# The last group's output stage: adds from bank C moved behind the fifth product, and two stores cut by column halves

## The chip, the cores and the metric

The kernel runs on one core of a Trainium2 chip. The metric is the device time of one execution in microseconds (us). The median of three runs before the change is 302.48 us (302.23 to 303.44).

## What is computed

Sliding-window causal attention over 8 batches, 8 heads, 576 positions and 64 values per head, followed by a feed-forward block on the joined heads:

```python
scores = scale * np.matmul(q, k.transpose(0, 1, 3, 2))      # window of 64, causal
attn   = softmax(masked scores)
x      = heads of attn @ v, side by side                    # [8, 576, 512]
xn     = (x - mu) / np.sqrt(var + 1e-06) * g_ln
ch     = np.maximum(xn @ w_ch1, 0.0) @ w_ch2                # 512 -> 2048 -> 512
out    = x + ch                                             # float32
```

## The kernel before, in words

The 8 x 576 rows are worked off in nine groups of 512 rows. Groups 0 to 7 hold the first 512 rows of one batch each. The ninth group, `g == NGRP - 1`, holds the last 64 rows of all eight batches: its block `kb` (128 rows, one row per SBUF partition) has the last 64 rows of batch `2*kb` in partitions 0 to 63 and those of batch `2*kb + 1` in partitions 64 to 127. The attention result of a block lies in `x_norm[(g, kb // 2)]`, a float32 tile of 128 partitions, 2 blocks and 512 columns; the feed-forward result is added into it in place, and it is stored from there.

The order on each engine is the order in which the program is written (the schedule is manual); nothing is reordered by a planner. Each engine works its own list from top to bottom and waits where an instruction needs another engine's result. Transfers are issued from SyncE's queue (SP) and from ScalarE's (ACT).

For the second matrix product of the block, groups from 2 on use a scheme of seven half-size products in the place of eight. The 512 rows are split in two halves of rows (blocks 0 and 1; blocks 2 and 3) and the 512 output columns in two halves of 256. Sums of the left factor's quarters, `S1` to `S4`, are made by VectorE (`s_sums`, L530); sums of the weights lie ready in `wT`. A product runs in two parts `p`, one per block, of 8 matmuls each, and goes to one of three sums in PSUM:

- bank A takes products 1, then 6, then 7 on top of one another
- bank B takes product 2, later product 4 anew
- bank C takes product 5, then product 3 on top. In the last group it is two separate banks of 256 columns, one per `p`

For the last group the plan runs the products in the order 1, 2, 6, 5, 7, 4, 3. As soon as a bank's sum is right for some part of the output, VectorE adds it into `x_norm` (`post`, L569, takes two blocks at 256 columns; `post_c`, L573, takes one block at 256 columns). A and C for the upper columns, A and B for the lower: blocks 2 and 3 get their upper 256 columns from product 7's A and product 5's C, and their lower 256 columns from product 7's A and product 4's B. Blocks 0 and 1 get their upper columns from product 6's A and product 3's C, which is the last sum of all. `stage(n, p)` runs one part of product `n` and then, after the second part, the adds and stores that it allows; `store_rest` (L511) issues two transfers, one from SP for partitions 0 to 63 and one from ACT for partitions 64 to 127 (or both from one given engine), for the two blocks and the given columns.

Between the parts of the products the plan writes the sums:

```python
stage(5, 0)
s_sums(0, 4, 4)
stage(5, 1)
s_sums(4, 8, 4)
for n in (7, 4, 3):
    for p in range(2):
        stage(n, p)
```

`S4`, of which the two calls here make the two halves, is the left factor of product 3.

Of the kernel before, what the change touches and what calls it, by code (L numbers as in the profile page):

```python
# [18 lines left out]
def kernel(  # L19
# [12 lines left out]
    DM = H * D  # L32
# [437 lines left out]
    def mlp_units(g, split=0, three=False, seven=True):  # L470
# [37 lines left out]
        def store_rest(k0, cols, eng):  # L508
            xv = x_norm[(g, k0 // 2)]
            for r in range(2):  # L510
                (eng or (nc.sync, nc.scalar)[r]).dma_start(  # L511
                    out=out[2 * k0 + r:2 * k0 + r + 3:2, SM:S, cols].rearrange("k s d -> s k d"),
                    in_=xv[64 * r:64 * r + 64, :, cols],
                )

        def store(kb):
            nc.sync.dma_start(out=out[g, 128 * kb:128 * kb + 128, :], in_=x_norm[(g, kb // 2)][:, kb % 2, :])
# [16 lines left out]
        def product(n, p):  # L534
            which, a, wv = {
                1: ("A", hv[:, :, 0, 0:256], w2v[:, :, 0, 0, :]),
                2: ("B", hv[:, :, 1, 0:256], w2v[:, :, 1, 0, :]),
                6: ("A", sS[2], wT[2]),
                5: ("C", sS[1], w2v[:, :, 0, 1, :]),
                7: ("A", sS[3], wT[3]),  # L540
                4: ("B", hv[:, :, 1, 256:512], wT[4]),
                3: ("C", sS[4], w2v[:, :, 1, 1, :]),
            }[n]
            first = n in (1, 2, 5, 4)
            if p == 0 and n in (1, 2 if last else 4, 5):
                if which == "C" and last:
                    for r in range(2):
                        bank[("C", r)] = ps_t.tile([128, 256], FP32, tag=f"t{r}", name=f"pC{r}_{g}")
                elif which == "C":
                    bank[which] = ps_t.tile([128, 2, 256], FP32, tag="t1", name=f"p{which}_{g}")  # L550
                else:
                    bank[which] = ps_mm.tile([128, 2, 256], FP32, tag="mm", name=f"p{which}_{g}")
            split_c = last and which == "C"
            o = bank[(which, p)][:, :] if split_c else bank[which][:, p, :]
            for c in range(NHC // 2):
                nc.tensor.matmul(  # L556
                    out=o, lhsT=a[:, c, 128 * p:128 * p + 128], rhs=wv[:, c, :],
                    start=(first and (p == 0 or split_c) and c == 0), stop=(c == NHC // 2 - 1), skip_group_check=True,
                )

        def post_both(which, kb0):
            xv = x_norm[(g, kb0 // 2)][:, :, :].rearrange("p k (f d) -> p k f d", f=2)
            a = bank[which][:, :, :]
            twice = bass.AP(tensor=a.tensor, offset=a.offset, ap=[a.ap[0], a.ap[1], [0, 2], a.ap[2]])
            nc.vector.tensor_tensor(out=xv, in0=twice, in1=xv, op=ALU.add)

        def post(which, kb0, f):
            xv = x_norm[(g, kb0 // 2)][:, :, 256 * f:256 * f + 256]
            nc.vector.tensor_tensor(out=xv, in0=bank[which], in1=xv, op=ALU.add)  # L569

        def post_c(kb0, r):
            xv = x_norm[(g, kb0 // 2)][:, r, 256:512]
            nc.vector.tensor_tensor(out=xv, in0=bank[("C", r)], in1=xv, op=ALU.add)  # L573

        last = g == NGRP - 1

        def stage(n, p):
            product(n, p)
            if last and n == 3:
                post_c(0, p)  # L580
                if p:
                    store_rest(0, slice(256, DM), None)
                return
            if p == 0:
                return
            if n == 1:
                post("A", 0, 0)
            elif n == 2:
                post("B", 0, 0)
                if last:  # L590
                    store_rest(0, slice(0, 256), nc.sync)
            elif n == 6:
                post("A", 0, 1)
            elif n == 5 and not last:
                post("C", 2, 1)
            elif n == 7 and last:
                post("A", 2, 1)
                post_c(2, 0)
                post_c(2, 1)
                post("A", 2, 0)  # L600
            elif n == 7:
                post_both("A", 2)
                store(2)
                store(3)
            elif n == 4:
                post("B", 2, 0)
                if last:
                    store_rest(2, slice(0, DM), None)
            elif n == 3:
                post("C", 0, 1)  # L610
                tbank["shared"] = False
                tbank["n"] = 0
                store(0)
                store(1)
# [109 lines left out]
        if last:  # L724
            def plan():
# [3 lines left out]
                for d in range(1, 4):  # L729
# [4 lines left out]
                    if d == 2:  # L734
                        s_sums(0, 4, 1)
                stage(1, 0)
                s_sums(0, 4, 2)
                l1_c(3)
                s_sums(4, 8, 1)
                stage(1, 1)  # L740
                l1_e(3)
                s_sums(4, 8, 2)
                stage(2, 0)
                stage(2, 1)
                stage(6, 0)
# [188 lines left out]
    for g in range(NGRP):  # L934
# [171 lines left out]
        n = g + 2  # L1106
# [75 lines left out]
```

## Time and profile before

| what | value |
|---|---|
| median of three runs | 302.48 us (302.23 to 303.44) |
| the profiled execution, its own time | 302.3 us |
| its span, first to last instruction | 300.3 us |
| TensorE busy | 292.2 us (97% of the span) |
| VectorE busy | 208.4 us (69%) |
| ScalarE busy | 153.9 us (51%) |
| GpSimd busy | 158.4 us (53%) |
| mean granted TensorE clock | 0.995 |
| last group's stores (L511) | 6 transfers: 4 from SP's queue, 2 from ACT's |

The profile is of one execution. Its times are counted from the span's start. PE is TensorE's matmul row, PEld its weight loads, DVE VectorE, ACT ScalarE, POOL GpSimd, SP SyncE; SPq and ACTq are the queues' issues of transfers. In a timeline row the columns are start, length, engine, line and operation, output and inputs, shape, and count; neighbouring instructions of one kind are merged, and what stands in brackets is idle time of the engine just before and what ended it. Ends of matmuls are modelled.

### The profile page before, as it was taken

Reading aid. Unit: us, or ns where it says so; the run is one execution under the profiler, and the core shown is the slowest. Engines: PE = TensorE matmul, PEld = TensorE weight load, DVE = VectorE, ACT = ScalarE, POOL = GpSimd, SP = SyncE. Lnnn points to the kernel's source line nnn. Section 1 sums busy time; section 2 is a strip of 40 time slices with the busy share of each in tenths; the row PEclk is TensorE's granted clock in tenths of the full one; section 3 lists DMA queues with packets and bytes.
Section 4 is the critical chain, followed back from the end, with each engine's and each line's share of the span. In section 5 each row is a group of like instructions: output and inputs, shape, how many; then the busy total and the mean of one; then the engine's idle time right before and its main releaser. Section 6 shows DMA issues by size and latency. Waiting matters only on the chain.

```text
span 300.3 us, 7568 instructions
## 1 busy us (share of the span) xinstructions
PE 292.2 (97%) x3067; PEld 195.6 (65%) x3067; DVE 208.4 (69%) x409; ACT 153.9 (51%) x259; POOL 158.4 (53%) x234
## 2 busy tenths in 40 slices
PE   8989999999999999999999999999999999999992
PEld 3557545887544588557854786469646854788881
DVE  1781338865937985488858865698667775879972
ACT  2666646676458525873276438841674056216400
POOL 4787877634633876278518860797048307115200
PEclk9999999999999999999999999999999999999997
DMA  7999999989979998999289999992639396013014
GB/s 191 260 382 335 384 286 289 269 266 306 134 194 297 206 187 128 290 248 177 53 265 289 195 160 270 297 163 48 212 72 157 70 232 146 10 38 121 0 38 105
DMA packets 114020, 58.34 MB, mean 194 GB/s; under 512 B 83649, under 2 KB 104705, under 8 KB 113986
## 3 DMA queue, kind: packets, MB, share of 16 engines
q1 hardware_dynamic: 113696, 57.47, 80.0%
q8 instruction: 24, 0.39, 0.6%
q10 hardware_dynamic: 290, 0.40, 0.5%
q14 instruction: 10, 0.08, 0.1%
HBM read 38.80 MB, written 9.44 MB: 161 GB/s over the span
## 4 chain that ended last, share of the span: by engine, by line
PE 95%; ACT 1%; DVE 1%; issue 0%
PE hps L479 31%; PE pA L556 12%; PE pB L556 8%; PE pC L556 8%; PE hph L621 7%; PE ch L491 6%; PE xps L387 4%; PE sc L340 4%; PE ch L638 4%; PE tp L267 3%; PE lA L677 2%; PE warm L848 2%; PE lC L677 1%; PE ztp L456 1%; PE lB L677 1%; ACT pt L350 1%
## 5 line engine op out<-in xcount | busy, mean ns | idle before, releaser
L479 PE MATMUL hps<-zT,w1g 128*128 128x512 f16 x416 | 94.7, 379 | 0.0
L483 ACT ACTIVATE hrT<-hps 128x512 f16<-128x512 f32 x104 | 62.3, 599 | 41.2 <-PE hps L479 37.8
L479 PEld LDWEIGHTS <-w1g 128*128 128x128 f16 x416 | 39.2, 98 | 45.5 <-issue 2.2
L350 ACT ACTIVATE pt<-sc 128x512 f16<-128x512 f32 x72 | 39.3, 600 | 21.4 <-PE sc L340 20.7
L556 PEld LDWEIGHTS <-sS 128*128 128x128 f16 x448 | 43.3, 98 | 5.0
L431 POOL TENSOR_SCALAR rsz<-mvg 128x1 f32<-128x1 f32 x28 | 9.7, 347 | 67.7 <-DVE mvg L412 65.7
L360 DVE TENSOR_TENSOR pt<-pt,mask 128x1024 f16<-128x1024 f16 x32 | 24.7, 776 | 22.3 <-ACT pt L350 22.3
L145 POOL CAST qk<-qk 128x1024 f16<-128x1024 f32 x30 | 33.0, 1114 | 10.3 <-PE hph L621 4.5
L556 PEld LDWEIGHTS <-hrT 128*128 128x128 f16 x336 | 32.1, 98 | 6.4 <-ACT hrT L483 1.0
L248 ACT COPY qkT<-tp 128x1024 f16<-128x1024 f16 (+1 forms) x18 | 17.4, 964 | 24.7 <-PE tp L267 22.4
L556 PE MATMUL pC<-w2s,sS 128*128 128x256 f16 x224 | 26.9, 273 | 0.0
L556 PE MATMUL pA<-wT,sS 128*128 128x256 f16 x224 | 26.9, 273 | 0.0
L407 DVE TENSOR_TENSOR xn<-xps,rcp 128x256 f32<-128x256 f32 (+1 forms) x50 | 25.8, 539 | 1.2 <-DMA out_dram<-xn 0.5
L409 DVE BATCH_NORM_STATS2 stats<-xn 128x6 f32<-128x512 f32 x36 | 25.0, 695 | 1.2
L530 DVE TENSOR_TENSOR sS<-hrT 128x512 f16<-128x512 f16 (+1 forms) x40 | 24.1, 604 | 1.9 <-ACT hrT L483 1.8
L621 PE MATMUL hph<-zT,w1g 128*128 128x256 f16 x192 | 23.4, 273 | 0.1
L437 POOL TENSOR_SCALAR z<-xn,rsz 128x512 f16<-128x512 f32 x24 | 20.7, 862 | 2.5
L403 DVE RECIPROCAL rcp<-xps 128x4 f32<-128x4 f32 (+1 forms) x50 | 7.9, 181 | 18.4 <-PE xps L387 18.4
L432 POOL TENSOR_TENSOR rsz<-rsz,mhalf 128x1 f32<-128x1 f32 x28 | 18.7, 670 | 2.3
L621 PEld LDWEIGHTS <-w1g 128*128 128x128 f16 x192 | 18.1, 98 | 2.9 <-issue 0.2
L491 PE MATMUL ch<-w2s,hrT 128*128 128x512 f16 x80 | 18.8, 380 | 0.0
L387 PEld LDWEIGHTS <-pt 128*64 128x64 f16 x576 | 11.6, 110 | 10.3 <-issue 6.0
(119 smaller groups left out, 427.9 us busy)
## 6 DMA issues: line engine op xcount, KB each, us to landing
out_dram<-xn SPq DMA_DIRECT2D x33, 256.0 KB, 3.2
qk<-in_q_dram SPq DMA_DIRECT2D x16, 512.0 KB, 6.2
qk<-in_k_dram SPq DMA_DIRECT2D x16, 512.0 KB, 7.2
v<-in_v_dram SPq DMA_DIRECT2D x28, 256.0 KB, 6.3
w2s<-in_moe_w_ch_dram SPq DMA_DIRECT2D x9, 512.0 KB, 8.6
w1s<-in_moe_w_ch_dram SPq DMA_DIRECT2D x4, 512.0 KB, 7.2
tk<-in_k_dram SPq DMA_DIRECT2D x8, 256.0 KB, 4.4
tv<-in_v_dram SPq DMA_DIRECT2D x8, 256.0 KB, 4.8
```

Source lines behind the costliest of these rows:

```text
L145: nc.gpsimd.tensor_copy(out=dst[:, :].rearrange("p (a j) e d -> p a e j d", j=j), in_=t[:, :].rearrange("p (a e j d) -> p a e j d", e=2, j ...
L350: nc.scalar.activation(out=o, in_=i, func=AF.Exp, bias=0.0, scale=scale)
L360: nc.vector.tensor_tensor(out=ptv, in0=ptv, in1=mb, op=ALU.mult)
L387: nc.tensor.matmul(out=tiles[h // n][64 * r:64 * r + 64, h % n, :D + 1], lhsT=pt[:, par, hp, r, :], rhs=rhs, start=True, stop=True)
L407: nc.vector.tensor_tensor(out=xn[:, n * i:n * i + n], in0=xps[:, :, 0:D], in1=rcp_b, op=ALU.mult)
L409: nc.vector.bn_stats(out=stats, in_=xv)
L479: nc.tensor.matmul(out=hps, lhsT=w1g[:, kc, 128 * hc:128 * (hc + 1)], rhs=zT[g][:, kc, :], start=(kc == 0), stop=(kc == NKC - 1),)
L483: nc.scalar.activation(out=hrT[:, hc, :], in_=hps, func=AF.Relu, bias=0.0, scale=1.0)
L491: nc.tensor.matmul(out=ch[kb], lhsT=hrT[:, hc, 128 * kb:128 * (kb + 1)], rhs=w2s[:, hc, :], start=(hc == 0), stop=(hc == NHC - 1),)
L530: nc.vector.tensor_tensor(out=o, in0=x, in1=y, op=op)
L556: nc.tensor.matmul(out=o, lhsT=a[:, c, 128 * p:128 * p + 128], rhs=wv[:, c, :], start=(first and (p == 0 or split_c) and c == 0), stop=(c ...
L621: nc.tensor.matmul(out=hps[:, e], lhsT=w1g[:, kc, 128 * hc:128 * (hc + 1)], rhs=zT[g][:, kc, 256 * half:256 * half + 256], start=(kc == 0) ...
```

## The change

In the last group, the two adds of C into blocks 2 and 3 are issued after the second part of product 5 and no longer after product 7. The store of these two blocks' 512 columns, which followed product 4's add, becomes two: the upper 256 columns are stored after product 7's first add, the lower 256 after product 4's add. Each is again one transfer from SP and one from ACT. Nothing else differs, in the other groups neither.

```diff
-            elif n == 5 and not last:
+            elif n == 5 and last:
+                post_c(2, 0)
+                post_c(2, 1)
+            elif n == 5:
                 post("C", 2, 1)
             elif n == 7 and last:
                 post("A", 2, 1)
-                post_c(2, 0)
-                post_c(2, 1)
+                store_rest(2, slice(256, DM), None)
                 post("A", 2, 0)
...
             elif n == 4:
                 post("B", 2, 0)
                 if last:
-                    store_rest(2, slice(0, DM), None)
+                    store_rest(2, slice(0, 256), None)
```

## The prediction

> **What bounds the kernel now.** I read the chain that ended last first, then the same chain for the last twelve microseconds, then the timeline there, and then the stores (issues with time to landing, and traffic by stretch). Over the whole span the chain is TensorE:
>
> ```profile
> PE 95%; ACT 1%; DVE 1%; issue 0%
> ```
>
> The change touches only the last group's output stage, so what counts is how that chain ends. From 289 us on it reads (start, length, what):
>
> ```profile
> 289.35 1.75 PE pA L556 x16
> 291.10 1.75 PE pB L556 x16
> 292.85 1.76 PE pC L556 x16
> 294.61 0.02 issue
> 294.63 0.42 DVE xn L573
> ```
>
> Products seven (pA), four (pB) and three (pC) run back to back, 1.75 us each; the last add follows 0.02 us after and ends at 295.05. No compute follows, but the span ends at 300.3: 5.25 us, about 1.7% of it, are stores. The timeline of that stage:
>
> ```profile
> 288.85 1.29 DVE L530 TENSOR_TENSOR sS<-hrT,sS 128x1024 f16<-128x1024 f16 x2
> 291.14 0.69 DVE L569 TENSOR_TENSOR xn<-pA,xn 128x512 f32<-128x512 f32 x1 [1.00 <-PE pA L556]
> 291.86 0.76 DVE L573 TENSOR_TENSOR xn<-pC,xn 128x256 f32<-128x256 f32 x2
> 292.54 0.68 DVE L569 TENSOR_TENSOR xn<-pA,xn 128x512 f32<-128x512 f32 x1
> 293.32 0.69 DVE L569 TENSOR_TENSOR xn<-pB,xn 128x512 f32<-128x512 f32 x1
> 293.93 0.41 DVE L573 TENSOR_TENSOR xn<-pC,xn 128x256 f32<-128x256 f32 x1
> 294.04 1.64 SPq L511 DMA_DIRECT2D out_dram<-xn  x2
> 294.04 1.91 ACTq L511 DMA_DIRECT2D out_dram<-xn  x2
> 294.63 0.42 DVE L573 TENSOR_TENSOR xn<-pC,xn 128x256 f32<-128x256 f32 x1 [0.28 <-PE pC L556]
> ```
>
> VectorE stands idle for 1.00 us before 291.14 and is then full until 294.34; the adds of blocks 2 and 3 from C (the two at 291.86) sit in the full part. Both halves of those rows go out at 294.04 in one pair of transfers (SP and ACT, 256 KB each), and the last pair (128 KB each) follows at 295.08. Of these four, in the order SP, ACT, SP, ACT (bytes each, us from issue to landing):
>
> ```profile
> out_dram<-xn SPq DMA_DIRECT2D x1, 256.0 KB, 3.2
> out_dram<-xn ACTq DMA_DIRECT2D x1, 256.0 KB, 4.5
> out_dram<-xn SPq DMA_DIRECT2D x1, 128.0 KB, 3.9
> out_dram<-xn ACTq DMA_DIRECT2D x1, 128.0 KB, 4.1
> ```
>
> The last lands at 295.08 + 4.1 = 299.2; 1.1 us of program end follow. SyncE's queue waits for exactly that:
>
> ```profile
> SPq L1177 <- DMA out_dram<-xn: 3.5, 1, 3.5
> ```
>
> And the transfers are busy, not merely late. By stretch (last two columns: share of the DMA engines, GB/s):
>
> ```profile
> 290.00:295.20 5.20, 4.59 (x43) 3.87 (x40) 3.63 (x8) 0.00 (x0) 0.00 (x0) 1.00 0.00 0
> 295.20:296.70 1.50, 0.00 (x0) 0.00 (x0) 0.00 (x0) 0.00 (x0) 0.00 (x0) 1.00 0.90 180
> 296.70:298.90 2.20, 0.00 (x0) 0.00 (x0) 0.00 (x0) 0.00 (x0) 0.00 (x0) 0.57 0.79 235
> ```
>
> For 5.2 us nothing moves; then 768 KB go in some 3.6 us, with the last pair queued behind the 512 KB of the pair before it. That queue is what the change can shorten.
>
> **The change, part by part.**
>
> *The two adds of C for blocks 2 and 3.* They move ahead of the second half of the last sum S4, to behind product five. Product five's end is product seven's start in the chain, 289.35. The first half of S4 fills VectorE until 288.85 + 0.64 = 289.5, so neither add waits; they take 0.76 us (their row at 291.86), and the second half of S4 ends at about 289.5 + 0.76 + 0.69 = 290.95 instead of 290.14. Behind it on VectorE is the add from A, due at 291.14, and still in time. The only other one who waits for S4 is product three, at 292.85: 1.9 us of slack, and PE loses nothing. The cover is the idle 1.00 us before 291.14; without it the 0.76 us would delay the A add as now, and reach PE only if more than 1.9 us.
>
> *VectorE behind product seven.* The A add for the upper half runs 291.14 to 291.83, as now. The A add for the lower half follows at once, 291.8 to 292.5. The add from B is then late on PE, not on VectorE: pB ends at 292.85, so it runs about 292.9 to 293.6 instead of 293.32 to 294.01. The first last C add needs half of product three (292.85 + 0.88 = 293.73) and the second needs all of it: 294.63 to 295.05, unchanged. So 0.76 us leave VectorE's full stretch and nothing of this reaches the last add; the worth of it is only the earlier release of stores.
>
> *The stores.* The pair of 256 KB becomes two pairs of 128 KB. The upper halves go at about 291.87, the lower halves at 293.6, the last pair at 295.08 as before. Added: one issue on SP's queue and one on ACT's, by their rows 0.6 us each on SP (two in 1.64 us with a gap) and up to 0.9 on ACT (two in 1.91). ACT's and SP's queues hold nothing else then, and the middle pair's issue ends by 294.5, 0.6 us ahead of the last one. Nobody waits behind them.
>
> *What the last pair finds in front of it.* Now 512 KB, issued 1.0 us earlier. Then 256 KB, issued 1.5 us earlier; the upper halves move in a stretch that shows 0 GB/s today. From issue to first bytes is about 1.2 us (294.04 to the traffic's start at 295.2). Two ways to price it:
> - By the row of a pair that finds nothing in front: its second half, ACT's 256 KB, landed after 4.5 us. A pair of half the size has 256 KB less to move, 1.46 us at 180 GB/s or 1.12 us at 235: landing after 3.0 to 3.4 us. Against 4.1 that is 0.7 to 1.1 us won. A 128 KB store of the same shape, issued alone at 286.61, landed after 3.2 us, which lies inside.
> - What may be taken off: the middle pair lands by the same figure at 293.6 + 3.0 to 3.4 = 296.6 to 297.0, and the last pair's first bytes come at 295.08 + 1.2 = 296.3. Some 0.0 to 0.4 us of queue stay, the landing itself including a receipt of about 0.3 us (traffic ends at 298.9, landing 299.2).
>
> So 0.3 to 1.1 us are won; I take 0.9, the 3.2 us of the nearest row (same shape and size). Sum: span 300.3 - 0.9 = 299.4, the profiled execution 302.3 - 0.9 = 301.4. That execution lies 0.2 us under the median of the runs, 302.48, so the median becomes 301.6.
>
> *Packets of half the length.* A row's run in DRAM falls from 2 KB to 1 KB. The pair at 286.61 has 1 KB runs; the stretch 287.9 to 289.7, which holds all its traffic, shows 146 GB/s at a DMA share of 0.64, against 180 at 0.90 for 2 KB runs. Per busy share that is 228 against 200: no loss shows. Bound: 256 KB at 146 GB/s, 1.8 us, against 1.46 at 180, so 0.3 us later for the last pair if it queues, which stays inside the 0.3 to 1.1.
>
> [...]
>
> **The rivals.**
>
> *The last landing does not move* (chance 0.18). ACT's transfer of a pair landed 1.3 us after SP's though both were issued at 294.04. If that lag belongs to the second queue and not to the bytes, the ACT half lands 4.1 us after 295.08 with whatever in front. For: ACT's lag also shows with an empty queue. Against: the last pair's lag is only 0.2 us. Time: 302.5.
>
> *More than a measurement can tell* (0.14). The lag is all queue, and with little in front the last pair lands as fast as the fastest store in the kernel: 2.0 us (the minimum over all output stores; median 3.3). Then 2.1 us are won: 300.4. Against: no store of the 64-row shape landed under 3.2.
>
> *Slower* (0.06). A transfer costs by its number, not its bytes: the first 256 KB transfer kept the engines from 295.2 to about 296.7, 1.5 us. Six transfers at 1.5 us in series from 293.1 (291.87 + 1.2) end at 302.1 instead of 298.9, 3.2 us later: 305.7. It decides from 0.97 us each (293.1 + 6 x 0.97 = 298.9). Against: the two transfers at 286.61 together fit in 1.8 us.
>
> That the change doesn't do what it says could only be that the early C adds wait for product five; by 289.35 against 289.5 they don't, and the slack of 1.9 us covers it.
>
> **How the numbers follow.** The forecast has 0.62. About 0.5% of the time, 1.5 us, is what a measurement of this kernel can tell from no change; that puts the bounds at 301.0 and 304.0. The forecast (301.4 to 302.2) and the first rival are within; 0.02 of the forecast's 0.62 may fall below 301.0 by scatter, while 0.01 of the rival "more" stays above it: faster 0.15. Slower by over 0.5% comes from the last rival alone, 0.06. Same is 0.79. Range: 300.6 to 302.8 holds the forecast and the first rival with the runs' scatter (302.23 to 303.44 before), and leaves out the two other rivals, 0.2.
>
> **What would show it.** Right: the chain's last C add still at 294.6, PE without a new gap before product three, traffic from about 293.1, a pair issued at 293.6, the last landing after 3.0 to 3.4 us. Wrong: PE waiting for S4, the first A add behind 291.2, the last issue later than 295.1, or a last landing still over 4 us with the lower halves gone by 297.

## The result and the profile after

The changed kernel takes 300.85 us (median of 6 runs, 300.71 to 301.32) against 302.42 us (6 runs, 302.23 to 303.44): ratio 0.9946, 95% interval 0.9931 to 0.9961. Run a second time later it took 300.76 us, ratio 0.9960 (0.9947 to 0.9974). The gain is 1.6 us by the medians, 1.4 us by the two profiled executions (302.3 and 300.89 us, spans 300.3 and 298.9).

The end of the chain of waits in the changed kernel (start, length, what):

```profile
291.02 1.75 PE pB L556 x16
292.76 1.76 PE pC L556 x16
294.53 0.02 issue
294.55 0.43 DVE xn L573
```

TensorE has no new gap; its products are 0.08 us earlier throughout, and that shift is older than the changed stage. The last add ends at 294.98 (295.05 before). The timeline of the stage:

```profile
288.77 0.68 DVE L530 TENSOR_TENSOR sS<-hrT,sS 128x1024 f16<-128x1024 f16 x1
289.37 0.75 DVE L573 TENSOR_TENSOR xn<-pC,xn 128x256 f32<-128x256 f32 x2
290.04 0.68 DVE L530 TENSOR_TENSOR sS<-hrT,sS 128x1024 f16<-128x1024 f16 x1
291.06 1.29 DVE L569 TENSOR_TENSOR xn<-pA,xn 128x512 f32<-128x512 f32 x2 [0.34 <-PE pA L556]
291.78 3.87 ACTq L511 DMA_DIRECT2D out_dram<-xn  x3
292.80 0.69 DVE L569 TENSOR_TENSOR xn<-pB,xn 128x512 f32<-128x512 f32 x1 [0.46 <-PE pB L556]
```

The two C adds (289.37) now sit between the halves of S4. The second half ends at 290.72, 2.0 us ahead of product three, and the add from A still waits for TensorE (0.34 us where it was 1.00). The add from B waits for TensorE, 0.46 us. ACT's three stores begin at 291.78. The traffic, by stretch (last two columns: share of the DMA engines, GB/s):

```profile
290.00:292.90 2.90, 2.90 (x29) 2.61 (x27) 2.11 (x5) 0.00 (x0) 0.00 (x0) 1.00 0.00 0
292.90:294.20 1.30, 1.30 (x14) 1.17 (x13) 1.02 (x2) 0.00 (x0) 0.00 (x0) 1.00 0.79 201
294.20:294.60 0.40, 0.31 (x3) 0.03 (x1) 0.05 (x1) 0.00 (x0) 0.00 (x0) 1.00 0.01 3
294.60:296.00 1.40, 0.00 (x0) 0.00 (x0) 0.38 (x1) 0.00 (x0) 0.00 (x0) 1.00 0.74 187
296.00:296.15 0.15, 0.00 (x0) 0.00 (x0) 0.00 (x0) 0.00 (x0) 0.00 (x0) 1.00 0.00 0
296.15:297.60 1.45, 0.00 (x0) 0.00 (x0) 0.00 (x0) 0.00 (x0) 0.00 (x0) 0.80 0.72 181
```

Three pairs of 256 KB, each over in 1.3 to 1.45 us, with quiet stretches between them (3 and 0 GB/s). The last pair finds nothing in front. Its landings, SP's and ACT's:

```profile
out_dram<-xn SPq DMA_DIRECT2D x1, 128.0 KB, 2.6
out_dram<-xn ACTq DMA_DIRECT2D x1, 128.0 KB, 2.9
```

They were 3.9 and 4.1 us. So the 1.4 us of the span are 0.07 (last pair issued at 295.01 instead of 295.08), 1.2 (landing 2.9 instead of 4.1) and 0.1 (1.0 us from the landing at 297.9 to the span's end, 1.1 before).

### The profile page after: what moved, and what is told of

It reads as the page before. It is cut to its first block, busy times and chain, and to the rows that moved or that the text cites. A ratio compares the mean times of both kernels' runs of the same rounds, so it can differ in the third digit from the quotient of the medians.

```text
span 298.9 us, 7573 instructions
## 1 busy us (share of the span) xinstructions
PE 292.1 (98%) x3067; PEld 195.4 (65%) x3067; DVE 207.7 (69%) x409; ACT 153.9 (52%) x259; POOL 159.7 (53%) x234
## 4 chain that ended last, share of the span: by engine, by line
PE 96%; ACT 1%; DVE 1%; issue 0%
PE hps L479 31%; PE pA L556 12%; PE pB L556 8%; PE pC L556 8%; PE hph L623 7%; PE ch L491 6%; PE xps L387 4%; PE sc L340 4%; PE ch L640 4%; PE tp L267 3%; PE lA L679 2%; PE warm L850 2%; PE lC L679 1%; PE ztp L456 1%; PE lB L679 1%; ACT pt L350 1%
## 5 line engine op out<-in xcount | busy, mean ns | idle before, releaser
L360 DVE TENSOR_TENSOR pt<-pt,mask 128x1024 f16<-128x1024 f16 x32 | 23.5, 740 | 22.2 <-ACT pt L350 22.2
L145 POOL CAST qk<-qk 128x1024 f16<-128x1024 f32 x30 | 34.0, 1148 | 9.1 <-DMA qk<-in_q_dram 5.9
L437 POOL TENSOR_SCALAR z<-xn,rsz 128x512 f16<-128x512 f32 x24 | 21.5, 897 | 2.5
```

The source lines that it names most:

```text
L145: nc.gpsimd.tensor_copy(out=dst[:, :].rearrange("p (a j) e d -> p a e j d", j=j), in_=t[:, :].rearrange("p (a e j d) -> p a e j d", e=2, j ...
L360: nc.vector.tensor_tensor(out=ptv, in0=ptv, in1=mb, op=ALU.mult)
```

## The experiments

Because the whole program shifts by a few tenths from one profile to the next, each trace is also read by its tail: from the end of the last add (its start plus its length) to the span's end. It is 5.25 us before (295.05 to 300.3) and 3.9 with the change (294.98 to 298.9).

Theory Q: the last pair landed late because 512 KB were moving in front of it. Rival D: VectorE's shorter work behind product seven carries the gain.

**The split without the move of the adds.**

Against the kernel before:

```diff
                 post_c(2, 0)
                 post_c(2, 1)
+                store_rest(2, slice(256, DM), None)
                 post("A", 2, 0)
...
                 if last:
-                    store_rest(2, slice(0, DM), None)
+                    store_rest(2, slice(0, 256), None)
```

> The store is split as in the change, but the two adds from C stay behind the A add, so the upper halves go out at about 292.65 us instead of 291.8. Theory Q (the last pair lands late because 512 KB are still moving in front of it): the upper 256 KB move in 293.9 to 295.1, the lower 256 KB (issued about 294.0) in 295.2 to 296.4, the last pair starts at about 296.4 and lands some 3.0 us after its issue; nearly the whole gain stays, span about 299.1, ratio 0.995 to 0.997. Rival D (the gain is VectorE's shorter full stretch): nothing is won, ratio 1.000.

Measured: 300.95 us, ratio 0.9948 (0.9936 to 0.9959), span 298.9, tail 4.1 us. Traffic by stretch:

```profile
293.65:294.95 1.30, 0.72 (x7) 0.40 (x5) 0.90 (x3) 0.00 (x0) 0.00 (x0) 1.00 0.80 202
294.95:296.20 1.25, 0.00 (x0) 0.00 (x0) 0.00 (x0) 0.00 (x0) 0.00 (x0) 1.00 0.82 207
296.20:297.60 1.40, 0.00 (x0) 0.00 (x0) 0.00 (x0) 0.00 (x0) 0.00 (x0) 1.00 0.68 190
```

The upper halves go 0.6 us later than in the change (issued at 292.42), yet all three pairs are through one after the other without a queue worth the name: the last pair lands after 2.8 and 3.0 us. Rival D, which gave 1.000, is out: the split alone gives the whole gain that the timing can see, and about 1.2 of the 1.35 us of tail.

**The move of the adds without the split.** Against the changed kernel:

```diff
-                store_rest(2, slice(256, DM), None)
                 post("A", 2, 0)
...
-                    store_rest(2, slice(0, 256), None)
+                    store_rest(2, slice(0, DM), None)
```

> The two adds from C move behind product five as in the change, but the rows of blocks 2 and 3 are stored whole, at about 293.55 us instead of 294.04. Theory Q: the last pair still queues behind 512 KB that began only 0.5 us earlier; its landing shrinks by at most those 0.5 us, from 4.1 to about 3.6 us, span about 299.8, ratio 0.998 to 0.9995. Rival D (VectorE's order carries the gain): ratio 0.995.

Measured: 301.95 us, ratio 0.9983 (0.9975 to 0.9992), span 299.8, tail 4.6 us. The issues, SP and ACT of the 512 KB pair and of the last one, and the traffic:

```profile
out_dram<-xn SPq DMA_DIRECT2D x1, 256.0 KB, 3.2
out_dram<-xn ACTq DMA_DIRECT2D x1, 256.0 KB, 4.2
out_dram<-xn SPq DMA_DIRECT2D x1, 128.0 KB, 3.2
out_dram<-xn ACTq DMA_DIRECT2D x1, 128.0 KB, 3.4
```

```profile
295.00:296.60 1.60, 0.00 (x0) 0.00 (x0) 0.20 (x1) 0.00 (x0) 0.00 (x0) 1.00 0.94 201
296.60:298.30 1.70, 0.00 (x0) 0.00 (x0) 0.00 (x0) 0.00 (x0) 0.00 (x0) 1.00 0.87 274
```

The store goes out 0.44 us earlier against the last pair (1.48 us ahead of it, 1.04 before), and the last landing falls by 0.7, to 3.4 us. That is more than the 0.5 us expected as the most; the second stretch of the traffic moved at 274 GB/s where that of the kernel before shows 235, and why was not found. The engines are busy without a break. Both parts of the change shorten one queue, so their gains don't add: 1.2 and 0.65 us of tail alone, 1.35 together.

**Nothing in front at all.** Here the changed kernel leaves out the store of blocks 2 and 3, so these rows of the output are not written.

```diff
-                store_rest(2, slice(256, DM), None)
...
-                if last:
-                    store_rest(2, slice(0, 256), None)
```

> Blocks 2 and 3 are not stored at all; the last pair finds empty queues. Theory Q as the changed kernel's trace shows it (its last pair starts after the middle pair has ended): the landing is the same 2.6 (SP) and 2.9 us (ACT), span 298.9 within 0.1, ratio 0.994 to 0.996; there is no more to win in front of the last pair. If something of the earlier transfers still costs (receipts, issue), the landing falls to 2.3 or less and the span by 0.5 more.

Measured: 300.88 us, ratio 0.9949 (0.9936 to 0.9962), tail 3.9 us.

```profile
296.30:297.65 1.35, 0.00 (x0) 0.00 (x0) 0.00 (x0) 0.00 (x0) 0.00 (x0) 1.00 0.77 194
```

The pair, alone, takes 1.35 us of traffic and lands after 2.5 and 2.8 us, as in the change within 0.1. The change has emptied the queue; the only way on is a smaller or earlier last pair.

**Half the bytes in front, with the 2 KB runs kept.** Rival R: the 1 KB runs of the split are what moves faster. From the kernel before, block 3 is left out of the store behind product four, and its rows are not written. `store_block` stores one block, partitions 0 to 63 from SP and 64 to 127 from ACT.

```diff
-                    store_rest(2, slice(0, DM), None)
+                    store_block(2, 0, slice(0, DM))   # block 2 alone, SP and ACT
```

> The kernel before with block 3 not stored: the pair in front of the last one is issued when it was (about 294.04 us) and has runs of 2 KB as it had, but 256 KB instead of 512. Theory Q (the bytes in front count): the last pair lands as in the kernel with the split alone, after 2.9 to 3.2 us instead of 4.1, ratio 0.995 to 0.9965. Rival R (the runs of 2 KB count, the split wins by its 1 KB runs): the landing stays near 3.7 us or above, ratio 0.9985 to 1.000.

Measured: 301.14 us, ratio 0.9960 (0.9947 to 0.9973), tail 4.0 us; the last pair lands after 2.6 and 2.9 us. The pair in front, 256 KB in 2 KB runs, shows 219 GB/s, the last pair, in 1 KB runs, 202:

```profile
295.20:296.40 1.20, 0.00 (x0) 0.00 (x0) 0.00 (x0) 0.00 (x0) 0.00 (x0) 1.00 0.82 219
296.40:297.70 1.30, 0.00 (x0) 0.00 (x0) 0.00 (x0) 0.00 (x0) 0.00 (x0) 1.00 0.74 202
```

Bytes in front, not the length of the runs, set the landing; R is out.

**The queues.** In the changed kernel's last pair SP's half moves first and slowly and ACT's follows fast: by the packets of the trace SP's 128 KB take 0.9 us (296.25 to 297.14, 148 GB/s on average) and ACT's 0.5 us (296.99 to 297.49, 266 GB/s). The expectations below take 165 and 350 GB/s, from short slices of that traffic. Three runs ask what the queues have to do with it. First the two queues change places:

```diff
-                (eng or (nc.sync, nc.scalar)[r]).dma_start(
+                (eng or (nc.scalar, nc.sync)[r]).dma_start(
```

> The changed kernel with partitions 0 to 63 issued from ACT and 64 to 127 from SP in all three pairs. In the changed kernel SP's half moves first and slowly (about 165 GB/s) and ACT's follows fast (about 350). If the slow one is slow because it is first (its descriptors are made while it moves), SP's stays first and slow whatever its rows. If the rows or partitions are slow, now ACT's half moves at 165. Either way time 300.8 within 0.4, ratio 0.994 to 0.996; if the slow half goes last, 0.3 us more.

Measured: 300.88 us, ratio 0.9945 (0.9932 to 0.9958), tail 3.9 us, landings 2.5 and 2.9 us, SP's still first. It is not the rows or the partitions. Then all three pairs from SP alone (`nc.sync` in the place of `None` in the three calls of the changed kernel):

> The changed kernel with both transfers of all three pairs issued from SP. If the second queue is worth something (its descriptors are made while SP's transfer moves), both transfers now move at some 165 GB/s and the second is issued 0.6 us later: the last landing is 2.9 us + 0.4 for the rate + up to 0.2, about 3.3 to 3.5 us after the first issue of the pair, span 299.4, ratio 0.996 to 0.998. If the queue does not matter: 0.995.

Measured: 301.36 us, ratio 0.9959 (0.9944 to 0.9975), span 299.4, but the last add itself ended 0.4 us later in this profile (295.40): the tail is 4.0 us. The last pair's traffic, in the changed kernel and here:

```profile
296.20:297.50 1.30, 0.00 (x0) 0.00 (x0) 0.00 (x0) 0.00 (x0) 0.00 (x0) 0.81 0.80 202
296.65:298.15 1.50, 0.00 (x0) 0.00 (x0) 0.00 (x0) 0.00 (x0) 0.00 (x0) 1.00 0.77 175
```

The same 256 KB take 0.2 us longer on one queue. The expectation of 3.3 to 3.5 us from the pair's first issue to the last landing missed: the second transfer, issued some 0.7 us behind the first, lands after 2.4 us, so it is about 3.1. By the tail, one queue costs 0.1 us more than two. And the last pair from ACT alone (`nc.scalar` in the last call):

> The changed kernel with both transfers of the last pair issued from ACT. If ACT's transfers are fast by themselves (350 GB/s without SP's in front), the first one is over 0.4 us after its first byte and the second, issued 0.65 us later, lands 2.5 to 2.7 us after the pair's first issue: span 298.6, ratio 0.993 to 0.995. If the first in a row is slow on any queue, it is as SP alone: landing 3.3 to 3.5 us, ratio 0.996 to 0.998.

Measured: 301.17 us, ratio 0.9956 (0.9942 to 0.9970), span 299.6 with the last add's end at 295.62, tail 4.0 us. The last pair's traffic:

```profile
296.90:298.40 1.50, 0.00 (x0) 0.00 (x0) 0.00 (x0) 0.00 (x0) 0.00 (x0) 0.96 0.78 175
```

Neither expectation holds in its numbers, but the tail and the traffic are those of SP alone, as the second one has it: ACT's transfers are not fast by themselves. Within a pair on two queues one half is slow and one fast; why was not found.

**Less in the last pair.** In the changed kernel block 0's upper columns are stored behind their own add, block 1's behind the last.

```diff
                 post_c(0, p)
-                if p:
-                    store_rest(0, slice(256, DM), None)
+                store_block(0, p, slice(256, DM))          # 64 KB from SP, 64 KB from ACT
                 return
```

> The changed kernel with the last pair of stores cut by blocks: block 0's upper columns go out behind its own add (about 294.15 us), block 1's behind the last add (295.0), 64 KB from SP and 64 KB from ACT each. Theory Q with what the runs showed since (SP's transfer moves at some 165 GB/s from 1.2 us after its issue, ACT's follows at some 350, and each pair ends before the next begins): block 1's pair has half the bytes, 0.6 us less to move; it lands 2.2 to 2.4 us after its issue instead of 2.9, span 298.3, ratio 0.992 to 0.994. Rival N (the number of transfers costs): the third and fourth pair collide (issues 0.6 us each, block 0's issue ends only at 294.8), the landing stays at 2.9 or more, ratio 0.995 or above.

Measured: 300.46 us, ratio 0.9928 (0.9915 to 0.9940), span 298.2, tail 3.4 us; ACT's last transfer lands 2.3 us after its issue. Rival N, the number of transfers, fell. To tell it from the change, both ran again side by side on one chip:

> The changed kernel itself, beside the next one on the same chip: ratio 0.9945 within 0.001, from the last add's end to the span's end 3.9 us.

> The kernel with the last pair cut by blocks again, to tell it from the change itself. Theory Q: block 1's pair has 128 KB less to move, 0.5 us less from the last add's end to the span's end than the change (3.4 us against 3.9), ratio 0.9925 to 0.9935. If the first comparison was scatter, the ratio is that of the change, 0.9945.

Measured: the change 300.76 us, ratio 0.9960 (0.9947 to 0.9974), tail 3.8 us; the last pair by blocks 300.47 us, ratio 0.9947 (0.9933 to 0.9960), tail 3.3 us. Both ratios came out higher than expected: 0.9947 would by itself be the value named for scatter, but the change beside it stood at 0.9960. Twice the version by blocks is 0.3 to 0.4 us under the change by the medians and 0.5 us by the tail, as the halved pair says; the intervals of the ratios overlap, so by the timing alone it is not settled.

## Why the prediction was right or wrong

- *The stores are what is left behind the last add, and the 512 KB in front set the last landing.* Right, and shown: halving those bytes without touching anything else (landing 2.9 us), splitting alone (3.0) and removing them (2.8) all give what the change gives.
- *VectorE and TensorE.* Right to 0.2 us: no wait for product five, second half of S4 at 290.72 (290.95 foretold), the add from B at 292.80, the last add unmoved, the pairs issued at 291.78, 293.53 and 295.01 (291.87, 293.6 and 295.1). The move of the adds alone won 0.17%, and with it the last add began 1.78 us behind product three's start, as in the kernel before: what the move wins is the earlier release.
- *The size, 0.9 us instead of 1.4 by the profiled executions (1.6 by the medians).* The term that was mis-sized is the landing of the last pair with nothing in front: 3.2 us taken, 3.0 to 3.4 worked out, 2.9 measured. It was worked out from ACT's 256 KB, 4.5 us, called a pair with nothing in front. But its last stretch ran beside the last pair's traffic from behind, so more than 256 KB had to come off; in the run of the adds alone, where the last pair came 0.44 us later behind it, the same transfer landed after 4.2. A better sum lay in the same trace: 1.2 us to the first bytes, 1.46 for 256 KB at 180 GB/s, and 0.3 from traffic's end to landing make 3.0; at the 201 GB/s that the pairs showed later it is 2.8. The store at 286.61, the nearest row, was not alone but the first of two on SP's queue, and slower than any of the new ones, 3.2 us against 2.5 or 2.6. The one queue is not the reason, for from SP alone the stores of the tail landed after 2.4 us; why it was slower stays open. The landing accounts for 0.3 of the 0.5 us that were missing; the rest is the last issue, 0.07 us earlier, and the program's end, 0.1 us shorter.
- *The 0.0 to 0.4 us of queue that might stay.* None stayed: the middle pair was over at 296.0 and the last began at 296.15.
- *Half-length runs.* No loss, as taken; the run with 2 KB runs shows 219 against 202 GB/s, which is 0.1 us for 256 KB and inside the bound of 0.3.
- *The rivals.* The lag of the second queue is not fixed: ACT's half lands 0.3 us behind SP's, not 1.3. The lowest store (2.0 us) was not reached, yet 1.4 us of the 2.1 were. A price by number is out: six transfers were over at 297.6, and eight (by blocks) end earlier still. The Trainium skill ("DMA: Bandwidth & Descriptors", section "Rules for kernel authors") says to coalesce many small transfers into a large one. Here the two added transfers cost nothing that the times show: the first pair moved from 292.90 to 294.20, where the kernel before shows 0 GB/s.
- *The border of 0.5%.* The change sits on it: 0.54% and 0.40% in two comparisons. The forecast gave 0.79 to "within 0.5%" and was too sure of that side: its 301.6 us lay only 0.6 us from the border at 301.0, and the gain was underrated by 0.5.
- *The range.* The gain is larger than the 0.3 to 1.1 us that the prediction worked out, the last landing shorter than the 3.0 to 3.4 it named as the sign of being right, and 300.85 us lies under its 301.4 to 302.2. It lies inside 300.6 to 302.8 only because that range was drawn 0.8 us wider at its lower end, for scatter. The mechanism was right; that the range held is in part luck.

## What to carry to other kernels

When a kernel ends in stores, look at the traffic between the last add and the end: if bytes that could have gone earlier are in front of the last transfer, release them earlier, even in smaller transfers, until the last one finds the engines quiet; then make the last one smaller (0.5 us of tail here, by the medians not settled). To price it, build the landing from its parts (issue to first bytes, bytes by the rate of a transfer alone, receipt), not by subtracting from a landing that overlaps with others. A new order of adds is worth what it releases: here 0.65 us of tail alone, and on top of the split only some 0.2 us of tail, which the ratios (0.9946 and 0.9948) don't show.

## What was not expected of the hardware

The Trainium skill ("DMA: Bandwidth & Descriptors", section "Rules for kernel authors") says that spreading transfers over issuing engines brings no bandwidth. The measurement says otherwise by a little: the last pair's 256 KB moved within 1.3 us from two queues and within 1.5 us from SP or from ACT alone, with tails of 3.9 and 4.0 us.

With 768 KB in one go the rate rises to 274 GB/s in the second half (adds alone), against 175 to 219 for a pair by itself. The size of a transfer alone does not set the rate, for ACT's 128 KB of a pair moved at 266 GB/s on average. What does set it was not tested.
